# A dummy first activation, and all four units of the first attention group scored in plain fp32

## The chip, the cores and the metric

The kernel runs on one core of one Trainium2 chip. The metric is the device time of one execution in microseconds; three runs of the kernel before the change had a median of 709.19 us (709.08 to 709.35).

## The reference

Three stages follow each other. Attention with a memory is computed for 2 batches, 8 heads, 576 rows and 64 columns a head; its output goes through a dense layer with an ELU between two weights, and this through four experts, each weighted by a probability of the row.

```python
scores = scale * np.matmul(q, k.transpose(0, 1, 3, 2))
scores = np.where(causal, -1000000000.0, scores)
a = np.exp(scores - scores.max(-1, keepdims=True))
a /= a.sum(-1, keepdims=True) + 1e-09
local = np.matmul(a, v)
q_p = phi(q)                              # phi(x) = where(x > 0, x, exp(x) - 1) + 1
mem_out = (q_p @ M_prev) / (q_p @ z_prev + 1e-6)
attn = g * mem_out + (1 - g) * local      # g = sigmoid(beta), one a head
...
h = x @ w_in                              # 1152 x 512 by 512 x 2048
x = np.where(h > 0.0, h, np.exp(np.minimum(h, 0.0)) - 1.0) @ w_out
...
for e in range(E):                        # 4 experts, 512 x 1024 x 512
    out += p[:, e:e + 1] * (np.maximum(x @ w1[e], 0.0) @ w2[e])
```

## The kernel before, in words

All work is cut into steps, each with an engine, a cost, a rank and the steps that it needs. A planner (`Plan.order`) walks a model of the five engines when the program is built, and of the steps that could start on an engine it takes the one with the lowest rank; what comes out is a fixed order of instructions on each engine. On the chip each engine runs its order strictly, one instruction after the other, and waits on semaphores for what it needs. The table `MOVES` shifts ranks by step or by family of steps (`("R", "load")` is the load of all units of kind R, `"R00"` all steps of one unit). `STAY` says how far down the ranks TensorE looks for a step of the kind that it is at (attention or dense layers) before it turns to the other kind; its first number holds while it is at attention. Nothing of the planner's costs is a time of the chip.

Attention is done in units of a pair of heads. Four units `F0` to `F3` hold the first 192 rows of both batches (tiles 0 and 1, 192 keys wide, and tile 2, 64 wide); their output is the input of the first token group (384 rows) of the dense layers. Eight units `R00` to `R13` hold the rest (tiles 576, 448 and 320 keys wide), for the second group of 768 rows. The steps of a unit are:

- `load` and `load_v`: the queries with the keys (tile `qk`), and the values with the memory (tile `rv`), issued by SyncE;
- `split_h` on ScalarE and `split_l` on GpSimd: a high part `qh` in fp32r, the reduced-precision type, and the rest `ql`; a unit in `DIRECT` leaves them out;
- `phi_r`, `phi_e`, `phi_p` on ScalarE and `phi` on GpSimd (for R, `phi_p` is GpSimd's too): phi of the queries, then `mem` on TensorE into the bank `om`;
- `score` on TensorE: three products of the parts (high by high, low by high, high by low), or one in plain fp32 for a `DIRECT` unit; the two heads go to two PSUM banks;
- `lowest` on VectorE: mask and minimum, with the result in SBUF; `exp` on ScalarE; `trans` on TensorE, four blocks at a time into the one bank `t`; `evac` copies them to SBUF, on ScalarE for even groups and on VectorE for odd ones; `values` on TensorE into the bank `ov`; then the quotient on VectorE, the sum with the memory part, the turn on TensorE, and the split of the result as input of the dense layer.

The weights come as 64-bit words for the first dense layer (steps `upper` on ScalarE, `shift` and `lower` on VectorE, for each half of a weight, put the words back into fp32; for the first three weights these work in the tile `wr` in SBUF, for the others in a PSUM bank), and as fp32 for the experts; `part_h` on ScalarE and `part_l` on GpSimd split them into `wh` and `wl`. Each dense product is three fp32r products (`mm3`). Tiles go round in rings: two each of `raw`, `qh`, `ql` and `rv`, one of `om`, `ov` and `t`. A load into a ring waits until the last reader of the tile that it replaces is done. Seven fillers (products of zeros, L342) run first on TensorE, and some more where the planner sees a wait or a unit of kind F begins a group.

Of the kernel before, what the change touches and what calls it, by code (L numbers as in the profile page):

```python
# [8 lines left out]
F32 = mybir.dt.float32  # L9
F32R = mybir.dt.float32r  # L10
I32 = mybir.dt.int32
I64 = mybir.dt.int64
AF = mybir.ActivationFunctionType
# [3 lines left out]
B, H, S, D = 2, 8, 576, 64  # L17
# [3 lines left out]
P = 128  # L21
# [6 lines left out]
NQ = 384  # L28
# [4 lines left out]
KEYS = {"F": 192, "R": 576}  # L33
# [20 lines left out]


MOVES = {
# [11 lines left out]
}  # L68


# [14 lines left out]
def f32(ap):  # L85
    return ap.bitcast(F32)
# [3 lines left out]
def tile_kernel(  # L90
# [12 lines left out]
    nc = tc.nc  # L103
    qk, vm = {"F": qk_f, "R": qk_r}, {"F": vm_f, "R": vm_r}

    const = ctx.enter_context(tc.tile_pool(name="const", bufs=1))
# [29 lines left out]
    zeros = const.tile([P, P], mybir.dt.bfloat16, name="zeros")  # L136
    nc.vector.memset(zeros, 0.0)


    wmem = const.tile([P, H], F32, name="wmem")  # L140
    wloc = const.tile([P, H], F32, name="wloc")
# [63 lines left out]
    UNIT1 = 5.0  # L205

    LANDING = 1.2
    DIRECT = ("F0", "F1")
    EARLY = 4.0
    START2 = 48.0  # L210
    STARTS2 = [0, 35, 70, 95, 110, 125, 140, 155]
# [143 lines left out]
    def atile(shape, dtype, tag, name):  # L355
        return at["sbuf"].tile(shape, dtype, tag=tag, name=name, bufs=SLOTS[tag])
# [719 lines left out]
    def act_cost(n, psum=False):  # L1076
        return 0.833e-3 * n + (0.055 if psum else 0.095)
# [4 lines left out]
    def pool_cost(n):  # L1082
        return 2.1e-3 * n + 0.2
# [2 lines left out]

        return 0.06 * (kind == "F") + 0.203 * sum(2 if kind == "F" and (t, odd) == (2, 2) else 1 for t, odd, _ in blocks)

    STAY = [16.5, 17.0]
    TURN = 0.09  # L1090

    def attends(key):
# [117 lines left out]
    def plan_unit(plan, kind, b, c, start, spare, slack):  # L1210
# [5 lines left out]
        widest = 1344  # L1216
        unit, uid = {}, f"F{c}" if kind == "F" else f"R{b}{c}"

        def parts_of(t):

            if kind == "F":
                return [(t, 0, P)] if t < 2 else [(0, 0, D), (1, D, D)]
            return [(0, 0, P)]

        def add(key, engine, cost, fn, after=(), takes=(), gives=()):
            step = key.rstrip("0123456789")
            plan.add(
                (uid, key), engine, cost, start + OFFSET[step], fn,
                [(uid, a) if isinstance(a, str) else a for a in after], takes, gives,
                slack.get(engine, 0.0) + LANDING * (step in ("split_h", "phi_r") and uid not in ("F0", "F1")),  # L1230
                early=EARLY if kind == "R" else 1e9,
            )


        def load(cs):
            if "k" not in unit:
                unit["k"] = atile([P, NQ + KEYS["R"]], F32, tag="raw", name=f"qk{uid}")[:, :nq + nk]
            nc.sync.dma_start(out=unit["k"][:, cs], in_=(qk[kind][c] if kind == "F" else qk[kind][b, c])[:, cs])

        def load_v():  # L1240
# [31 lines left out]
        whole, direct = slice(0, nq + nk), uid in DIRECT  # L1272
        if uid == "F0":

            add("load_k", "sync", 0.8, lambda: load(slice(nq, nq + nk)), takes=["raw"])
            add("load_q", "sync", 0.5, lambda: load(slice(0, 2 * P)))
            add("load", "sync", 0.4, lambda: load(slice(2 * P, nq)))
        else:
            add("load", "sync", 1.6, lambda: load(whole), takes=["raw"])
        add("load_v", "sync", 1.3, load_v, takes=["rv"])  # L1280
        if not direct:
            n = nq + nk
            add("split_h", "act", act_cost(n), lambda: split_h(whole), ["load"], ["qh"])
            add("split_l", "pool", pool_cost(n), lambda: split_l(whole), ["split_h"], ["ql"])
        add("phi_r", "act", act_cost(nq), phi_r, ["load"], ["pp"])
        add("phi_e", "act", act_cost(nq), phi_e, ["phi_r"], ["pe"])
        if kind == "F":
            add("phi_p", "act", act_cost(nq), phi_p, ["phi_e"] + ["split_l"] * (not direct), gives=["raw"] * (not direct))
            add("phi", "pool", pool_cost(nq), phi, ["phi_p"] + ["score20"] * direct, gives=["pe"] + ["raw"] * direct)
        else:  # L1290
            add("phi_p", "pool", 2.5e-3 * nq + 0.2, phi_p, ["phi_e"])
            add("phi", "pool", pool_cost(nq), phi, ["phi_p", "split_l"], gives=["raw", "pe"])
# [108 lines left out]
            nc.scalar.activation(out=blk, in_=blk, func=AF.Exp, scale=-1.0, bias=unit["nm"][odd][:, k:k + 1])  # L1401

        def score_cost(t, w):
            return len(parts_of(t)) * max((4 if direct else 3) * w / 2400, 0.32) + 0.24 + 0.22 * FEWEST[kind] * (t != 1)

        for t, n, a, z_ in pieces:
            first, last = (t, n) == pieces[0][:2], (t, n) == pieces[-1][:2]
# [265 lines left out]
```

## Time and profile before

| | |
|---|---|
| median of 3 runs | 709.19 us |
| the profiled execution | 709.2 us |
| its span, first to last instruction | 707.4 us |
| TensorE busy | 696.5 us, 98% |
| GpSimd, VectorE, ScalarE busy | 424.3, 388.5, 350.9 us |
| granted TensorE clock over the span | 1.000 |

The span is the time between the first and the last instruction of the profiled execution; 1.8 us of its time lie around it. Busy times of the engines overlap. A matmul's end is modelled in the profile, so that consecutive matmuls overlap in the rows: the time from one start to the next is the better price. A bracket at the end of a row of the timeline holds the idle time before it and who ended it.

### The profile page before, as it was taken

Reading aid. Unit: us, or ns where it says so; the run is one execution under the profiler, and the core shown is the slowest. Engines: PE = TensorE matmul, PEld = TensorE weight load, DVE = VectorE, ACT = ScalarE, POOL = GpSimd, SP = SyncE. Lnnn points to the kernel's source line nnn. Section 1 sums busy time; section 2 is a strip of 40 time slices with the busy share of each in tenths; the row PEclk is TensorE's granted clock in tenths of the full one; section 3 lists DMA queues with packets and bytes.
Section 4 is the critical chain, followed back from the end, with each engine's and each line's share of the span. In section 5 each row is a group of like instructions: output and inputs, shape, how many; then the busy total and the mean of one; then the engine's idle time right before and its main releaser. Section 6 shows DMA issues by size and latency. Waiting matters only on the chain.

```text
span 707.4 us, 10617 instructions
## 1 busy us (share of the span) xinstructions
PE 696.5 (98%) x4043; PEld 636.6 (90%) x4043; DVE 388.5 (55%) x844; ACT 350.9 (50%) x607; POOL 424.3 (60%) x255
## 2 busy tenths in 40 slices
PE   8989999999999999999999999999999999999997
PEld 5778998899888898999999999999898989989896
DVE  3897787553445323523727557763554636355462
ACT  6878967664434523544855546733332424233220
POOL 4877767566553444598886464796645666464210
PEclk9999999999999999999999999999999999999999
DMA  7889986433322331234321202122220303111002
GB/s 275 281 273 306 311 301 223 173 99 109 117 93 63 118 116 63 90 120 156 111 77 60 90 30 62 60 91 81 66 90 30 120 11 110 58 62 60 0 1 89
DMA packets 23826, 82.19 MB, mean 116 GB/s; under 512 B 2912, under 2 KB 3296, under 8 KB 23776
## 3 DMA queue, kind: packets, MB, share of 16 engines
q1 hardware_dynamic: 23776, 81.53, 34.9%
q8 instruction: 31, 0.51, 0.3%
q14 instruction: 19, 0.16, 0.1%
HBM read 70.77 MB, written 10.75 MB: 115 GB/s over the span
## 4 chain that ended last, share of the span: by engine, by line
PE 83%; DVE 0%; issue 0%
PE db L318 9%; PE db L316 9%; PE db L317 9%; PE da L316 4%; PE da L318 4%; PE da L317 4%; PE ub L316 3%; PE ub L318 3%; PE ub L317 3%; PE ov L1457 3%; PE sR L1378 2%; PE tR L1441 2%; PE ov L1464 1%; PE pb17S L318 0%; PE pb16S L317 0%; PE pb15S L316 0%
## 5 line engine op out<-in xcount | busy, mean ns | idle before, releaser
L284 POOL TENSOR_TENSOR wl<-wr,wh 128x1024 fp32r<-128x1024 f32 x72 | 172.1, 2395 | 161.0 <-ACT wh L280 152.5
L280 ACT ACTIVATE wh<-wr 128x1024 fp32r<-128x1024 f32 x72 | 76.0, 1056 | 114.4 <-PE db L317 73.0
L316 PE MATMUL db<-wh,hb 128*128 128x512 f32 x288 | 112.8, 392 | 0.0
L318 PE MATMUL db<-wl,hb 128*128 128x512 f32 x288 | 112.5, 391 | 0.0
L317 PE MATMUL db<-wh,hb 128*128 128x512 f32 x288 | 112.4, 390 | 0.0
L1046 DVE SCALAR_TENSOR_TENSOR acc<-db,pr,acc 128x512 f32<-128x512 f32 x42 | 31.5, 751 | 70.8 <-PE db L318 70.8
L316 PE MATMUL da<-ha,wh 128*128 128x384 f32 x192 | 65.9, 343 | 0.0
L318 PE MATMUL da<-ha,wh 128*128 128x384 f32 x192 | 64.3, 335 | 0.0
L318 PEld LDWEIGHTS db<-wl,hb 128*128 128x128 f32 x288 | 54.0, 188 | 11.4
L317 PE MATMUL da<-ha,wl 128*128 128x384 f32 x192 | 64.2, 335 | 0.0
L316 PEld LDWEIGHTS db<-wh,hb 128*128 128x128 f32 x288 | 54.1, 188 | 10.7 <-issue 0.2
L317 PEld LDWEIGHTS db<-wh,hb 128*128 128x128 f32 x288 | 54.1, 188 | 10.7
L316 PE MATMUL ub<-yh,wh 128*128 128x384 f32 x128 | 45.2, 353 | 0.0
L318 PE MATMUL ub<-yl,wh 128*128 128x384 f32 x128 | 43.0, 336 | 0.0
L317 PE MATMUL ub<-yh,wl 128*128 128x384 f32 x128 | 43.0, 336 | 0.0
L1457 PE MATMUL ov<-rvR,pfR 128*128 128x65 f32 x288 | 38.5, 265 | 0.0
L1457 PEld LDWEIGHTS ov<-rvR,pfR 128*128 128x128 f32 x288 | 37.7, 191 | 0.7 <-issue 0.2
L554 ACT ACTIVATE hb<-ub 128x384 fp32r<-128x384 f32 x32 | 15.7, 491 | 43.5 <-PE ub L318 43.1
L316 PEld LDWEIGHTS da<-ha,wh 128*128 128x128 f32 x192 | 36.1, 188 | 1.0 <-issue 1.0
L557 DVE SCALAR_TENSOR_TENSOR hb<-ub,hb 128x384 fp32r<-128x384 f32 x32 | 17.7, 557 | 33.4 <-ACT hb L554 33.4
L317 PEld LDWEIGHTS da<-ha,wl 128*128 128x128 f32 x192 | 36.1, 188 | 0.0
L318 PEld LDWEIGHTS da<-ha,wh 128*128 128x128 f32 x192 | 36.0, 188 | 0.0
(859 smaller groups left out, 1820.6 us busy)
## 6 DMA issues: line engine op xcount, KB each, us to landing
wr<-in_w SPq DMA_DIRECT2D x64, 512.0 KB, 3.5
w<-in_w SPq DMA_DIRECT2D x32, 512.0 KB, 6.3
wscr<-wr SPq DMA_DIRECT2D x16, 512.0 KB, 7.2
wr<-wscr SPq DMA_DIRECT2D x16, 512.0 KB, 3.3
rvR<-in_vm_r SPq DMA_DIRECT2D x8, 520.0 KB, 4.5
qkR<-in_qk_r SPq DMA_DIRECT2D x8, 480.0 KB, 6.2
rvF<-in_vm_f SPq DMA_DIRECT2D x4, 520.0 KB, 5.0
out<-acc SPq DMA_DIRECT2D x8, 256.0 KB, 2.0
```

The costliest lines, as they stand in the source:

```text
L280: nc.scalar.activation(out=t["wh"], in_=t["wr"], func=AF.Copy)
L284: nc.gpsimd.tensor_tensor(out=wl, in0=t["wr"], in1=f32(t["wh"]), op=ALU.subtract)
L316: nc.tensor.matmul(out, ah, bh, start=first, stop=False)
L317: nc.tensor.matmul(out, al, bh, start=False, stop=False)
L318: nc.tensor.matmul(out, ah, bl, start=False, stop=last)
L554: nc.scalar.activation(out=t["h"][:, 0], in_=t["ps"], func=AF.Relu)
L557: nc.vector.scalar_tensor_tensor(out=t["h"][:, 1], in0=t["ps"], scalar=0.0, in1=f32(t["h"][:, 0]), op0=ALU.max, op1=ALU.subtract)
L1046: nc.vector.scalar_tensor_tensor(out=acc, in0=t["ps"], scalar=p, in1=acc, op0=ALU.mult, op1=ALU.add)
L1378: nc.tensor.matmul(unit["s", odd, t, n][:, :w], unit[x][rows, q], unit[y][rows, ks[odd]], start=m == 0 and r0 == 0, stop=m == len(terms) - ...
L1441: nc.tensor.transpose(pst[:, P * n:P * n + P], src, ident)
L1457: nc.tensor.matmul(unit["ov"][:, odd, t], pf[:, col:col + P], unit["rv"][:, at_], start=False, stop=odd == 1 and j == nb - 1)
L1464: nc.tensor.matmul(pair("ov", t, r0, r), pf[:, col + r0:col + r0 + r], apart(at_), start=True, stop=nb == 0,)
```

## The change

ScalarE gets a first operation, an exponential of one column of the tile of zeros that the fillers use. `F2` and `F3` join the units that score in plain fp32, so their `split_h` and `split_l` and their buffers `qh` and `ql` are not needed; their raw tiles (queries and keys) are laid into these two rings in place of `raw`. The planner's costs for these scores, two costs of phi on ScalarE, `STAY` and the whole table `MOVES` are changed with it, and so the order of the program on every engine.

```diff
 MOVES = {
-    ("F", "exp"): 15.5, ("F", "load"): -18.5, ("F", "trans"): 3, ("F0", "mem"): 5.5, ("F0", "values1"): 17,
...
+    ("F", "exp"): 9.8, ("F", "score"): -61.6, ("F", "turn"): 30.9, ("F1", "exp21"): -1.6,
...
+    awake = const.tile([P, 1], F32, name="awake")
+    nc.scalar.activation(out=awake, in_=zeros[:, :1], func=AF.Exp)
...
-    DIRECT = ("F0", "F1")
+    DIRECT = ("F0", "F1", "F2", "F3")
...
-    STAY = [16.5, 17.0]
+    STAY = [145.4, 17.7]
...
+        home = {"F2": "qh", "F3": "ql"}.get(uid, "raw")
...
-                unit["k"] = atile([P, NQ + KEYS["R"]], F32, tag="raw", name=f"qk{uid}")[:, :nq + nk]
+                block = atile([P, NQ + KEYS["R"]], F32 if home == "raw" else F32R, tag=home, name=f"qk{uid}")
+                unit["k"] = f32(block)[:, :nq + nk]
...
-            add("load", "sync", 1.6, lambda: load(whole), takes=["raw"])
+            add("load", "sync", 1.6, lambda: load(whole), takes=[home])
...
-        add("phi_e", "act", act_cost(nq), phi_e, ["phi_r"], ["pe"])
+        add("phi_e", "act", act_cost(nq) + 0.12, phi_e, ["phi_r"], ["pe"])
...
-            add("phi_p", "act", act_cost(nq), phi_p, ["phi_e"] + ["split_l"] * (not direct), gives=["raw"] * (not direct))
-            add("phi", "pool", pool_cost(nq), phi, ["phi_p"] + ["score20"] * direct, gives=["pe"] + ["raw"] * direct)
+            add("phi_p", "act", act_cost(nq) + 0.12, phi_p, ["phi_e"] + ["split_l"] * (not direct), gives=["raw"] * (not direct))
+            add("phi", "pool", pool_cost(nq), phi, ["phi_p"] + ["score20"] * direct, gives=["pe"] + [home] * direct)
...
-            return len(parts_of(t)) * max((4 if direct else 3) * w / 2400, 0.32) + 0.24 + 0.22 * FEWEST[kind] * (t != 1)
+            if direct:
+
+                cold = {0: 0.7, 1: 0.35}.get(t, 0.0) * (uid == "F0")
+                return len(parts_of(t)) * (0.32 if w > D else 0.25) + 0.12 + 0.05 * (t == 2) + 0.22 * FEWEST[kind] * (t != 1) + cold
+            return len(parts_of(t)) * max(3 * w / 2400, 0.32) + 0.24 + 0.22 * FEWEST[kind] * (t != 1)
```

ScalarE at the start of the program, before: `pp` and `pe` are the tiles of phi, `pt` holds scores and then exponentials, `pf` the copies of transposed blocks `t`; the name's first letters after it are the unit.

```order
L1257 ACT_TABLE_LOAD
L1257 ACTIVATE ppF0_155<-qkF0_139 128x448
L1261 ACTIVATE peF0_163<-ppF0_155 128x448
L1265 ACTIVATE ppF0_155<-qkF0_139 128x448
L1401 ACTIVATE ptF0_147<-ptF0_147,nmF00_148 128x192
L1257 ACTIVATE ppF1_180<-qkF1_143 128x448
L1401 ACTIVATE ptF0_147<-ptF0_147,nmF01_149 128x192
L1401 ACTIVATE ptF0_147<-ptF0_147,nmF00_148 128x192
L1401 ACTIVATE ptF0_147<-ptF0_147,nmF01_149 128x192
L1401 ACTIVATE ptF0_147<-ptF0_147,nmF00_148 128x64
```

The same place after the change:

```order
L143 ACT_TABLE_LOAD
L143 ACTIVATE awake_95<-zeros_93 128x1
L1266 ACTIVATE ppF0_157<-qkF0_141 128x448
L1270 ACTIVATE peF0_161<-ppF0_157 128x448
L1274 ACTIVATE ppF0_157<-qkF0_141 128x448
L1410 ACTIVATE ptF0_149<-ptF0_149,nmF00_150 128x192
L1410 ACTIVATE ptF0_149<-ptF0_149,nmF01_151 128x192
L1410 ACTIVATE ptF0_149<-ptF0_149,nmF00_150 128x192
L1410 ACTIVATE ptF0_149<-ptF0_149,nmF01_151 128x192
L1266 ACTIVATE ppF1_188<-qkF1_147 128x448
```

The table load stands at an operation on the zeros, F0's four 192-wide exponentials follow each other, and the first step of F1's phi has gone behind them. The copy `pfF00` (not in these rows) stands two exponentials and no other step further down.

SyncE's issues, from the first half of weight 0 on, before (`w64_i_h` is half h of weight i):

```order
L246 DMA w64_0_0_183<-in_w64 128x512
L1238 DMA qkF2_208<-in_qk_f 128x832
L246 DMA w64_0_1_230<-in_w64 128x512
L246 DMA w64_1_0_252<-in_w64 128x512
L1238 DMA qkF3_267<-in_qk_f 128x832
L246 DMA w64_1_1_290<-in_w64 128x512
L1242 DMA rvF2_315<-in_vm_f 128x1040
L1238 DMA qkR00_330<-in_qk_r 128x960
```

And after:

```order
L1247 DMA qkF2_182<-in_qk_f 128x832
L252 DMA w64_0_0_200<-in_w64 128x512
L1247 DMA qkR00_229<-in_qk_r 128x960
L252 DMA w64_0_1_242<-in_w64 128x512
L1251 DMA rvF2_264<-in_vm_f 128x1040
L171 DMA pr_99<-in_probs 128x36
L1247 DMA qkR10_298<-in_qk_r 128x960
L1247 DMA qkF3_322<-in_qk_f 128x832
```

F2's load and R00's have moved up, F3's has moved back behind R10's and F2's values, and weight 1 (not in these rows) comes behind F3.

VectorE around the minimum steps of unit R00, before: the rows `ISA pt...` are the minimum steps (each with a second row that reads out the minimum), `L270` is `lower`, `sR00001` and `sR00101` the scores of the second piece of the widest tile:

```order
L1392 ISA ptR00_537,nmR000_538<-sR00001_577,mask_71,nmR000_538 128x288
L1392 ISA nmR000_538 128x1
L1392 ISA ptR00_537,nmR001_539<-sR00101_578,mask_71,nmR001_539 128x288
L1392 ISA nmR001_539 128x1
L270 SCALAR_TENSOR_TENSOR wr1_324<-w64_1_1_290,wr1_324 128x512
L266 TENSOR_SCALAR cv3_0_599<-cv3_0_599 128x512
L270 SCALAR_TENSOR_TENSOR wr3_598<-w64_3_0_426,cv3_0_599 128x512
L1300 SCALAR_TENSOR_TENSOR nv_F3_630<-ov_121,wloc_96 128x6
```

And after:

```order
L1401 ISA ptR00_479,nmR000_480<-sR00001_523,mask_71,nmR000_480 128x288
L1401 ISA nmR000_480 128x1
L1401 ISA ptR00_479,nmR001_481<-sR00101_524,mask_71,nmR001_481 128x288
L1401 ISA nmR001_481 128x1
L1459 COPY pfF31_550<-tF31_537 128x384
L272 TENSOR_SCALAR wr1_461<-wr1_461 128x512
L276 SCALAR_TENSOR_TENSOR wr1_461<-w64_1_0_350,wr1_461 128x512
L1401 ISA ptR00_479,nmR000_480<-sR00010_555,mask_71 128x448
```

Behind the same minimum steps there stood three steps of weights, F3's quotient and more before R00's 448-wide piece (`sR00010`); now there stand one copy and two steps of weight 1, whose first half comes later than it did, and then that piece.

## Rows read from the trace of the kernel before

**Rows 1.** The page: span and TensorE's busy time, share and instructions.

```profile
span 707.4 us, 10617 instructions
PE 696.5 (98%) x4043; PEld 636.6 (90%) x4043; DVE 388.5 (55%) x844; ACT 350.9 (50%) x607; POOL 424.3 (60%) x255
```

**Rows 2.** Windows: length, busy PE, PEld, DVE, ACT, POOL, clock, DMA share, GB/s.

```profile
0.00:5.00 5.00, 4.03 (x12) 1.54 (x14) 0.11 (x1) 0.00 (x0) 3.20 (x14) 1.00 0.52 136
5.00:30.00 25.00, 23.30 (x195) 16.80 (x191) 16.47 (x72) 23.18 (x51) 14.44 (x9) 1.00 0.88 299
30.00:60.00 30.00, 27.23 (x203) 23.33 (x202) 26.96 (x64) 24.54 (x46) 24.18 (x18) 1.00 0.87 285
60.00:120.00 60.00, 58.31 (x383) 55.07 (x382) 47.36 (x101) 48.17 (x84) 43.19 (x27) 1.00 0.85 293
120.00:700.00 580.00, 580.00 (x3247) 537.15 (x3245) 296.14 (x606) 255.03 (x429) 339.30 (x190) 1.00 0.25 81
700.00:707.40 7.40, 3.63 (x17) 2.66 (x15) 1.50 (x2) 0.00 (x0) 0.00 (x0) 1.00 0.26 99
```

**Rows 3.** Timeline of ScalarE: start, duration, line, operation, tiles, count, idle before.

```profile
5.37 1.28 ACT L1257 ACT_TABLE_LOAD   x1 [5.37 <-DMA qkF<-in_qk_f]
6.66 0.58 ACT L1257 ACTIVATE ppF<-qkF 128x448 f32<-128x448 f32 x1
...
8.36 0.44 ACT L1401 ACTIVATE ptF<-ptF,nmF 128x192 f32<-128x192 f32 x1
```

**Rows 4.** Timeline of TensorE, units F0 and F1.

```profile
7.69 0.81 PE L342 MATMUL sF<-zeros 128*128 128x512 bf16 x3 [0.43 <-DVE nmF L1392]
8.43 0.92 PE L1378 MATMUL sF<-qkF 64*128 64x192 f32 x8
9.28 0.39 PE L342 MATMUL tF<-zeros 128*128 128x512 bf16 x1
9.75 0.93 PE L1441 MATMUL tF<-ident,ptF 128*128 128x128 f32 x4
...
13.08 0.49 PE L1464 MATMUL ov<-rvF,pfF 128*128 128x130 f32 x2 [0.72 <-ACT pfF L1448]
```

**Rows 5.** Timeline of ScalarE and GpSimd: split of a unit, one each.

```profile
15.00 0.88 ACT L1247 ACTIVATE qhF<-qkF 128x832 fp32r<-128x832 f32 x1
...
23.66 1.95 POOL L1252 TENSOR_TENSOR qlF<-qkF,qhF 128x832 fp32r<-128x832 f32 x1
```

**Rows 6.** Timeline of TensorE: F2's 192-wide scores from parts, and what follows.

```profile
21.24 0.36 PE L1378 MATMUL sF<-qhF 64*128 64x192 f32 x2
...
22.08 0.61 PE L342 MATMUL om<-zeros 128*128 128x512 bf16 x2
```

**Rows 7.** Timeline of TensorE: F2's turn and two long waits.

```profile
35.76 0.49 PE L1502 MATMUL xF<-ident,tvF 128*128 128x128 f32 x3
...
39.63 0.47 PE L1378 MATMUL sR<-qhR 64*128 64x448 f32 x2 [1.34 <-DVE wr L270]
...
51.21 0.66 PE L1441 MATMUL tR<-ident,ptR 128*128 128x128 f32 x4 [1.43 <-DVE pfR L1446]
```

**Rows 8.** Timeline of VectorE: `lower` of weights in SBUF.

```profile
35.75 2.43 DVE L270 SCALAR_TENSOR_TENSOR wr<-w,wr 128x512 int32<-128x512 int32 x1
...
45.21 2.63 DVE L270 SCALAR_TENSOR_TENSOR wr<-w,wr 128x512 int32<-128x512 int32 x1
...
48.53 0.69 DVE L270 SCALAR_TENSOR_TENSOR wr<-w,wr 128x512 int32<-128x512 int32 x1
```

**Rows 9.** Timeline of GpSimd: subtractions beside the two slow steps.

```profile
35.38 2.25 POOL L1252 TENSOR_TENSOR qlR<-qkR,qhR 128x960 fp32r<-128x960 f32 x1
...
45.03 2.27 POOL L1252 TENSOR_TENSOR qlR<-qkR,qhR 128x960 fp32r<-128x960 f32 x1 [2.33 <-ACT qhR L1247]
```

**Rows 10.** DMA issues from 0 to 40 us: size, median us to landing.

```profile
w<-in_w SPq DMA_DIRECT2D x10, 512.0 KB, 6.6
...
qkF<-in_qk_f SPq DMA_DIRECT2D x3, 416.0 KB, 4.0
```

More of the change, by code (lines that the diff above doesn't have):

```diff
@@ L1273, in plan_unit @@
         if uid == "F0":
-            add("load_k", "sync", 0.8, lambda: load(slice(nq, nq + nk)), takes=["raw"])
+            add("load_k", "sync", 0.8, lambda: load(slice(nq, nq + nk)), takes=[home])
             add("load_q", "sync", 0.5, lambda: load(slice(0, 2 * P)))
```

23 rows, old and new, of the table MOVES are left out of this document.

## The prediction

> **What bounds the kernel now.** I read the page first, then the table of windows, then the timelines of the first 60 us. TensorE is busy for 696.5 of the span's 707.4 us [rows 1], so the time can fall only where TensorE stands idle, or where its own work shrinks. The windows say where it stands idle [rows 2]: 0.97 us before 5 us (nothing to multiply yet), 1.70 us between 5 and 30, 2.77 between 30 and 60, 1.69 between 60 and 120, nothing from 120 to 700, and 3.77 at the end, where the last sums are formed and stored. What can be won are the middle three, 6.16 us. In 5 to 30 us ScalarE is the busiest engine beside TensorE (23.2 of 25 us), and the DMA engines run at 0.88; from 30 to 60 us VectorE is (27.0 of 30) [rows 2].
>
> The profiled execution took 709.2 us, that is 1.8 us around its span of 707.4 [rows 1]; the median of the timed runs is 709.19, so the same sum serves for both. What tells this kernel from no change is about 0.2%, 1.4 us.
>
> **The change, part by part.**
>
> *ScalarE's first operation.* Now ScalarE loads its table when its first operation's data have landed, at 5.37 us, for 1.28 us, and the first activation begins at 6.66 [rows 3]. The new operation reads a tile of zeros that VectorE sets at the start, so the table load goes into time in which ScalarE has nothing else to do, and the first activation can begin at 5.37. Gain on ScalarE: 1.28 us. The Trainium skill ("ScalarE: Activation LUTs", What ACT_TABLE_LOAD costs) adds a drain of about 1.38 us to a load of 1.28; here the activation follows the load at once, so the trace does not agree, and with the drain the sum would fall by up to 1.4 us more.
>
> What waits for it: F0's transposes on TensorE, which now start at 9.75 us [rows 4] behind F0's exponentials. In the new order the four exponentials stand in a row behind the three steps of phi. The first went at 8.36 [rows 3], so now at about 7.1; four of 0.44 us end by 8.8 at the latest, and the transposes can start at about 8.9, some 0.9 us sooner. But F1's scores, which stood ahead of these transposes (8.43 to 9.28 us), come behind them now. F0's scores end at 7.26 (7.69 less the 0.43 of waiting [rows 4]); two fillers follow, some 0.25 us each by the three that take from 7.69 to 8.43, and then TensorE idles from 7.7 to 8.9, about 1.2 us. Behind that the 0.72 us at 13.08 [rows 4], a wait for the copy of F0's transposes, should go: this copy is ScalarE's next step but two behind the exponentials. The walk down the new order gives about 1.2 us of idle time for 5 to 30 us in place of 1.70: **-0.5** (bounds: all 1.7 gone; or F0's transposes as late as now with nothing ahead of them, +0.9, which is 9.75 less 8.9).
>
> *F2 and F3 score in plain fp32.* Off TensorE, each drops one ScalarE copy of 0.88 us and one GpSimd subtraction of 1.95 us [rows 5], so F2's scores wait for its load alone. On TensorE a pair of 192-wide tiles goes from 12 reduced-precision products to 4 plain ones. The 12 take from 21.24 to 22.08, 0.84 us [rows 6]; F1's 4 plain ones take from 8.43 to 9.28, 0.85 us [rows 4], at the full clock (1.00, 2.4 GHz [rows 2]). I take the cost as zero. It lies on the bounding engine, with no cover: if a group's price were wrong by 0.1 us, the four such groups of F2 and F3 (a 192-wide and a 64-wide one in each) would add 0.4. The Trainium skill ("FP8 and Floating Point Precision", TensorE Precision Notes) speaks against the change: true fp32 makes four passes through the array, while the split form makes three products. By that rule these four groups, at 0.84 us or less each, would cost up to a third more, at most 1.1 us, and the sum would be 707.9; the rows agree with no such loss, so I keep zero.
>
> *The raw tiles in the place of the split parts.* F2's load waited for F0's raw tile; its new buffer is free from the start, so its issue moves up in the queue. F0's values now come ahead of F1's keys, so F1 lands later by about the time of one more transfer (520 KB at the 299 GB/s of that window, 1.8 us [rows 2]); its cover is that F1's scores stand behind F0's transposes now. Without the cover the 1.8 us would be TensorE's. F3's load stands behind R10's, which needs F1's raw tile, and so F1's last scores: a new wait, and a rival below.
>
> *The new order between 30 and 60 us.* This is the largest term. The two long idle stretches are 1.34 us at 39.63 and 1.43 at 51.21 [rows 7]. Both stand behind VectorE's step `lower` of an early weight, which took 2.43 us at 35.75 and 2.63 at 45.21, while the same step on the same shape took 0.69 at 48.53 [rows 8]. What differs is GpSimd: its subtractions of 2.25 and 2.27 us run at just those times [rows 9]. Such a stretch costs VectorE 1.7 to 1.9 us, and the minimum step behind it holds the PSUM banks of R00's next scores. In the new order the first of these `lower` steps stands ahead of the minimum steps of R00's 448-wide piece, not behind the scores that wait for them; between those scores and the next there stand F2's turn, F3's last values and six products of the first layer, which now take from 35.76 to 38.29 us (39.63 less the wait [rows 7]), so 1.9 us of lateness is covered. The next two (weight 2) stand before the copy of R00's second transposes; there the cover is less, about 1 us. That GpSimd lost two subtractions of 2 us before this point makes a collision less likely, not impossible. I take one collision, half covered: 0.9 us of idle time in place of 2.77, **-1.9** (bounds: -2.8 with none; +2.7 with three uncovered, as the first rival has it).
>
> *60 to 120 us.* The order changes there too: units R00 to R11 are more tightly packed, since the kernel stays with attention as long as a step is ready. I found no wait there that goes or comes for certain, and take the 1.69 us as they are: **0** (bounds -1.7 to +1.7, none or twice as much). Entering another kind of product costs TensorE little: I count 56 entries of the dense layers from the plain fp32 products before and 48 now, and the scores' entries stay about as many; I take zero, within 0.5.
>
> *The rest of the table.* From 120 to 700 us TensorE has no idle time [rows 2], so reordering weights there is covered by TensorE itself; the end is not touched.
>
> Sum: 709.2 - 0.5 - 1.9 = **706.8 us**.
>
> **The rivals.**
>
> *VectorE falls under GpSimd (slower).* The place is the three `lower` steps in SBUF ahead of R00's minimum steps and transposes. If all three run beside a GpSimd subtraction, they cost 1.74, 1.94 and about 1.84 more, 5.5 us in all; if the tighter attention leaves TensorE nothing else to do, idle time between 30 and 60 us is 5.5 in place of my 0.9, and the time is 706.8 + 4.6 = 711.4. It is slower from 4.7 us of uncovered lateness on (710.6). For it: two of such steps fell so in the profile. Against: GpSimd has less to do before. Chance 0.13.
>
> *The waits only change place (no change).* Attention in a row makes a chain transposes, copy, values with one transposition bank; each link waits for a copy, and 6.2 us of idle time comes back elsewhere: 709.2. For it: TensorE's work stays the same, and VectorE was busy for nine tenths of 30 to 60 us. Chance 0.19.
>
> *F3's load is late.* By the walk its issue is at about 15 us, behind F1's last scores, and its own scores are due at 22. Such loads took 4.0 us to land, weights' 6.6 [rows 10]; beyond 7 us each further us is idle. At 10 us of landing it costs 3 and the time is 709.8; chance 0.05, half of it within the bound and half above it.
>
> *More than forecast.* All idle time between 5 and 120 us goes: 709.2 - 6.2 = 703.0. Chance 0.09; it asks that no collision is left.
>
> **How the numbers follow.** The forecast, 704.5 to 708, has 0.54. Faster: 0.54 + 0.09 = 0.63. Same: 0.19 and half of 0.05, 0.21. Slower: 0.13 and the other half, 0.16. The range runs from 702.9, which leaves out the lowest few of a hundred, to 710.6, above which lie most of the first rival and little else. For the forecast alone the range is 704.5 to 708.
>
> **What would show it.** Right: the table load ends before 3 us and the first activation begins at about 5.4; F0's transposes begin at 8.7 to 9.1; F2's and F3's pairs of 192-wide scores take 0.8 to 0.9 us; TensorE's idle time is about 1.2 between 5 and 30 us, and about 1 between 30 and 60, with its busy time within 1 us of 696.5. Wrong: a wait of over 1 us on VectorE's `lower` or on a copy of transposes between 30 and 65 us; a wait of F3's scores on its load at 22 us; idle time of over 3 us between 60 and 120 us, where I walked nothing; or scores in plain fp32 over 1 us a pair.

## The result, and the profile after

The changed kernel takes 702.25 us (median of 5 runs, 702.08 to 703.13), before 709.19 in the same session: ratio 0.9904, 95% interval 0.989 to 0.9919. It is faster, as forecast, but by 7 us where 2.4 were forecast, and 0.65 us below the wider of its two ranges (702.9 to 710.6).

The page of after, first line and engines, as [rows 1]:

```profile
span 700.3 us, 10577 instructions
PE 694.2 (99%) x4028; PEld 636.1 (91%) x4028; DVE 383.9 (55%) x844; ACT 349.2 (50%) x606; POOL 418.2 (60%) x253
```

The windows of after, columns as in [rows 2]:

```profile
5.00:30.00 25.00, 23.62 (x194) 16.93 (x192) 17.30 (x79) 22.15 (x52) 12.61 (x9) 1.00 0.91 305
30.00:60.00 30.00, 30.00 (x221) 26.38 (x218) 25.78 (x73) 25.18 (x46) 21.86 (x17) 1.00 0.88 290
60.00:120.00 60.00, 60.00 (x409) 56.84 (x408) 48.27 (x105) 47.56 (x84) 40.89 (x26) 1.00 0.85 296
```

TensorE's idle time went from 1.70 to 1.38 us (5 to 30 us), from 2.77 to 0 (30 to 60) and from 1.69 to 0 (60 to 120): 4.78 us. Its busy time fell by 2.35, from 696.5 to 694.15. Together that is the 7.1 us by which the span is shorter.

ScalarE's and TensorE's timelines of after at the start, as [rows 3, 4]:

```profile
0.72 1.28 ACT L143 ACT_TABLE_LOAD   x1 [0.72 <-PEq L1676]
2.01 0.20 ACT L143 ACTIVATE awake<-zeros 128x1 f32<-128x1 bf16 x1
5.38 0.58 ACT L1266 ACTIVATE ppF<-qkF 128x448 f32<-128x448 f32 x1 [3.16 <-DMA qkF<-in_qk_f]
7.08 1.48 ACT L1410 ACTIVATE ptF<-ptF,nmF 128x192 f32<-128x192 f32 x4
```

```profile
4.39 0.92 PE L1387 MATMUL sF<-qkF 64*128 64x192 f32 x8
8.01 0.93 PE L1454 MATMUL tF<-ident,ptF 128*128 128x128 f32 x4 [0.94 <-ACT ptF L1410]
...
20.00 0.66 PE L1387 MATMUL sF<-qkF 64*128 64x64 f32 x8
20.59 0.66 PE L1470 MATMUL ov<-rvF,pfF 128*128 128x65 f32 x4
...
22.53 0.92 PE L1387 MATMUL sF<-qkF 64*128 64x192 f32 x8
23.38 0.39 PE L348 MATMUL om<-zeros 128*128 128x512 bf16 x1
```

The table load lies in idle time, F0's transposes begin at 8.01 instead of 9.75 us [rows 4], and a pair of 192-wide plain fp32 scores of F3 takes 0.85 us from start to start (22.53 to 23.38), against 0.84 for the three products of parts [rows 6]. A pair of 64-wide ones takes 0.59 us (F2's, 20.00 to 20.59); before, F2's from parts took 0.79, from the first of these rows to the second:

```profile
24.44 0.30 PE L1378 MATMUL sF<-qhF 64*128 64x64 f32 x2
...
25.23 0.39 PE L342 MATMUL tF<-zeros 128*128 128x512 bf16 x1
```

VectorE's `lower` steps in SBUF, and GpSimd's timeline around them, as [rows 8, 9]:

```profile
34.03 0.69 DVE L276 SCALAR_TENSOR_TENSOR wr<-w,wr 128x512 int32<-128x512 int32 x1
36.65 0.69 DVE L276 SCALAR_TENSOR_TENSOR wr<-w,wr 128x512 int32<-128x512 int32 x1
43.32 0.68 DVE L276 SCALAR_TENSOR_TENSOR wr<-w,wr 128x512 int32<-128x512 int32 x1
44.38 0.69 DVE L276 SCALAR_TENSOR_TENSOR wr<-w,wr 128x512 int32<-128x512 int32 x1
```

```profile
32.72 1.00 POOL L1279 TENSOR_TENSOR ppR<-peR,ppR 128x384 f32<-128x384 f32 x1
37.04 1.33 POOL L1276 TENSOR_SCALAR ppR<-qkR 128x384 f32<-128x384 f32 x1 [3.32 <-ACT peR L1270]
38.52 2.39 POOL L290 TENSOR_TENSOR wl<-wr,wh 128x1024 fp32r<-128x1024 f32 x1
40.86 1.01 POOL L1279 TENSOR_TENSOR ppR<-peR,ppR 128x384 f32<-128x384 f32 x1
45.86 1.16 POOL L1276 TENSOR_SCALAR ppR<-qkR 128x384 f32<-128x384 f32 x1 [3.99 <-ACT peR L1270]
```

Almost all of each `lower` step falls into GpSimd's two gaps (to 37.04 and to 45.86 us), and all take 0.68 to 0.69 us. No collision of a `lower` step is left there, and neither are the waits of 1.34 and 1.43 us [rows 7].

### The profile page after: what moved, and what is told of

It reads as the page before. It is cut to its first block, busy times and chain, and to the rows that moved or that the text cites. A ratio compares the mean times of both kernels' runs of the same rounds, so it can differ in the third digit from the quotient of the medians.

```text
span 700.3 us, 10577 instructions
## 1 busy us (share of the span) xinstructions
PE 694.2 (99%) x4028; PEld 636.1 (91%) x4028; DVE 383.9 (55%) x844; ACT 349.2 (50%) x606; POOL 418.2 (60%) x253
## 4 chain that ended last, share of the span: by engine, by line
PE 97%; ACT 1%; DMA 1%; DVE 0%; SPq 0%; issue 0%; ACTq 0%
PE db L322 9%; PE db L324 9%; PE db L323 9%; PE da L322 5%; PE da L324 5%; PE da L323 5%; PE ov L1470 5%; PE ub L322 3%; PE ub L324 3%; PE ub L323 3%; PE sR L1387 3%; PE tR L1454 3%; PE ua L322 2%; PE ua L324 2%; PE ua L323 2%; PE ov L1477 1%
## 5 line engine op out<-in xcount | busy, mean ns | idle before, releaser
L1410 ACT ACTIVATE ptR<-ptR,nmR 128x576 f32<-128x576 f32 (+2 forms) x48 | 29.8, 662 | 11.3 <-DVE nmR L1401 11.2
```

## The experiments

The kernels whose expectations were worked out against the changed kernel's 702.25 us are compared with it by their medians; the ratios are against the kernel before, run in the same session each time. By the intervals of the ratios a difference of two medians is uncertain by 1 to 1.5 us, so that a difference of 1 us or less is an indication only.

**The dummy activation alone, in the kernel before.**

```diff
+    awake = const.tile([P, 1], F32, name="awake")
+    nc.scalar.activation(out=awake, in_=zeros[:, :1], func=AF.Exp)
```

> The kernel before, with only the dummy first activation added; the order of everything else is as before. Theory A (the new order made the gain; the table load alone is worth what TensorE's start waits for): F0's transposes start up to 0.25 us sooner, since F1's scores still stand ahead of them until 9.28 us and a filler behind, and the 0.72 us wait at 13.08 shrinks; the time is 708.0 to 709.0. Theory B (ScalarE was the bound of the first 30 us, so what is taken off it comes through in full): 1.28 us and more, 707.9 or less.

Measured: 707.98 us, ratio 0.9982 (0.9971 to 0.9994). The whole schedule moves up by about 1 us; both long waits stand where they stood in the order, and as long:

```profile
38.57 0.47 PE L1381 MATMUL sR<-qhR 64*128 64x448 f32 x2 [1.36 <-DVE wr L273]
50.12 0.66 PE L1444 MATMUL tR<-ident,ptR 128*128 128x128 f32 x4 [1.43 <-DVE pfR L1449]
```

By the ratio the early load brings 1.3 us (0.4 to 2.1), about its own length; the time lies at the border of the two theories.

**A collision taken out of the kernel before.** GpSimd waits with a subtraction until VectorE is past a `lower` step.

```diff
+            if (i, half) in ((1, 1), (2, 0)):
+                nc.vector.memset(flag[:, :1], 0.0)
...
+            if uid in ("R10", "R01"):
+                nc.gpsimd.tensor_copy(flag[:, 1:], flag[:, :1])
```

> The kernel before, with GpSimd's subtractions for R10 and R01 made to wait for the `lower` step of VectorE that they ran beside (weight 1's second half, weight 2's first), by a flag of one column that VectorE sets behind it; no step is moved. Theory A (the two long waits of TensorE came from these two slow steps): both steps take 0.7 us, the waits of 1.34 and 1.43 us shrink by 1.3 each at most, and the time is 706.5 to 708. Rival (VectorE was late for other reasons, or GpSimd's later end costs as much): 708.7 to 710.

Measured: 707.53 us, ratio 0.9971 (0.9961 to 0.9982). VectorE's first flagged `lower` step, and the step behind the second:

```profile
36.24 0.69 DVE L272 SCALAR_TENSOR_TENSOR wr<-w,wr 128x512 int32<-128x512 int32 x1
...
45.32 2.76 DVE L272 SCALAR_TENSOR_TENSOR wr<-w,wr 128x512 int32<-128x512 int32 x1
```

The first is free and its wait of 1.34 us is gone; at the second the subtraction, now from 45.28 us on, only met the next `lower` step, and 1.27 us of waiting stays. One collision removed is worth 2 us (1.3 to 2.7): its wait of 1.34 us, and a rest that this run does not explain.

**The split work put back, unread, in the changed kernel**: both halves, ScalarE's alone, GpSimd's alone. The order of everything else is that of the changed kernel, and nothing is left out.

```diff
+            if uid in ("F2", "F3"):
+                nc.scalar.activation(out=scratch, in_=unit["k"], func=AF.Copy)
...
+            if uid in ("F2", "F3"):
+                nc.gpsimd.tensor_tensor(out=scratch, in0=unit["k"], in1=scratch, op=ALU.subtract)
```

> The changed kernel, in the same order, with the split work of F2 and F3 put back as work whose result nobody reads: a ScalarE copy of 832 columns ahead of phi_r, and a GpSimd subtraction of 832 columns ahead of phi, for each of the two units. TensorE still scores from the raw tile. Theory A (order): this work had slack in the new order; the time is 702.2 to 703.3. Theory B (less work on ScalarE and GpSimd made the gain): 0.88 us on ScalarE and 2 us on GpSimd come back twice, and TensorE idles between 15 and 35 us: 704.5 to 707.

> The changed kernel with one ScalarE copy 832 wide put back for F2 and for F3, whose result nothing reads (the GpSimd half of the dropped split stays away). Both halves together took 704.3 us. Theory A (ScalarE was the engine that mattered: its queue stands ahead of the exps and copies that TensorE waits for): 703.5 to 704.5 us. Theory B (GpSimd's subtractions mattered, they delay what VectorE and TensorE need): 702.0 to 702.8 us.

> The changed kernel with one GpSimd subtraction 832 wide put back for F2 and for F3, whose result nothing reads (no copy on ScalarE). Theory A (ScalarE was the engine that mattered): 702.0 to 702.8 us. Theory B (GpSimd's subtractions mattered): 703.5 to 704.5 us, with waits of TensorE behind GpSimd, or behind VectorE where a step with two SBUF operands meets the subtraction.

Measured: 704.28 (ratio 0.9928, 0.9913 to 0.9943), 703.27 (0.9918, 0.9903 to 0.9933) and 703.76 us (0.9925, 0.991 to 0.994). The first lies just under B, the second between its theories, the third in B. ScalarE's half costs 1.0 us, of which its profile shows 0.47 as a late load (below), GpSimd's 1.5, of which 0.84, and both 2.0, of which 0.91. VectorE beside GpSimd with both halves:

```profile
20.06 1.76 DVE L273 TENSOR_SCALAR wr<-wr 128x512 int32<-128x512 int32 x1
21.86 1.50 DVE L277 SCALAR_TENSOR_TENSOR wr<-w,wr 128x512 int32<-128x512 int32 x1
```

```profile
19.59 1.95 POOL L1283 TENSOR_TENSOR scratch<-qkF,scratch 128x832 f32<-128x832 f32 x1
21.49 1.32 POOL L1284 TENSOR_TENSOR ppF<-peF,ppF 128x448 f32<-128x448 f32 x1
```

The same two steps with ScalarE's half alone:

```profile
20.06 0.95 DVE L273 TENSOR_SCALAR wr<-wr 128x512 int32<-128x512 int32 x1
21.05 0.69 DVE L277 SCALAR_TENSOR_TENSOR wr<-w,wr 128x512 int32<-128x512 int32 x1
```

So a subtraction that the change drops would itself be a collision in the new order: the shift meets it, `lower` meets the addition that it has delayed, VectorE is 1.6 us later, and TensorE, about to score F3, waits 1.08 us at 23.56 behind F2's last minimum step. ScalarE's half alone brings neither. This is weight 0, in the first 30 us. Between 30 and 60 us, where the collisions of the kernel before were, the kernel with both halves put back has almost no idle time on TensorE, and of its `lower` steps of weights 1 and 2 only the first is slow, beside an addition (ScalarE's half alone makes it as slow):

```profile
30.00:60.00 30.00, 29.73 (x219) 25.58 (x217) 25.34 (x70) 26.44 (x50) 22.47 (x16) 1.00 0.82 266
```

```profile
35.58 1.38 DVE L277 SCALAR_TENSOR_TENSOR wr<-w,wr 128x512 int32<-128x512 int32 x1
38.89 0.69 DVE L277 SCALAR_TENSOR_TENSOR wr<-w,wr 128x512 int32<-128x512 int32 x1
```

**Collisions put back at weights 1 and 2 of the changed kernel.**

```diff
+            if 0 < i < W_EARLY:
+                nc.vector.memset(flag[:, :1], 0.0)
+                nc.gpsimd.tensor_copy(flag[:, 1:], flag[:, :1])
+                nc.gpsimd.tensor_tensor(out=scratch, in0=wide, in1=wide, op=ALU.subtract)
```

> The changed kernel, but for weights 1 and 2 VectorE sets a flag ahead of each `lower` step, and GpSimd, which waits for that flag, runs a subtraction of two 896-wide SBUF tiles beside it (its result is read by nothing). In the trace of before a `lower` step beside such a subtraction took 2.4 to 2.6 us in place of 0.69. Theory A (the collisions on VectorE were priced rightly, and the new order has no cover for them): the `lower` steps of the two weights become 2.4 to 2.7 us, TensorE waits again behind VectorE between 30 and 60 us, 703.5 to 706 us. Theory B (the new order leaves VectorE enough slack, the collisions of before mattered only because other work was late there): the steps are just as long, TensorE does not wait, 702.0 to 703.0 us.

Measured: 703.78 us, ratio 0.9915 (0.9898 to 0.9933). The waits of TensorE that it brought:

```profile
PE ua L330 <- POOL wl L297: 0.9, 1, 0.9
PE da L330 <- POOL wl L297: 0.2, 1, 0.2
```

The time is A's, the mechanism is not: three of the four `lower` steps take 1.0 to 2.1 us (less than the 2.4 to 2.7 that were meant), and TensorE never waits for VectorE there. The cover that the prediction counted (the six products and F3's last values) was enough for these; what is late is GpSimd's own `wl`, behind the added work in its queue.

**One half of the change each: the old table and `STAY` with four units in plain fp32, and the new table with two; and the new table with the old `STAY`.**

```diff
-    STAY = [145.4, 17.7]
+    STAY = [16.5, 17.0]
...
-    DIRECT = ("F0", "F1", "F2", "F3")
+    DIRECT = ("F0", "F1")
```

> The changed kernel with the table and the STAY of the kernel before: fp32 scores in all four units, the dummy activation and the new homes stay, the scheduler orders them by the old numbers (62 filler matmuls where the changed kernel has 36). Theory A (the removed work and the early table load bring the larger half of the 7 us whatever the order): 703 to 705.5 us. Theory B (the new order brings the larger half): 706 to 709 us, with waits of TensorE of 3 us or more between 5 and 120 us.

> The changed kernel with its new table and its dummy activation, but F2 and F3 split again as before, their raw tiles in the raw buffers. The scheduler, told of the splits, makes its own order from the same table (54 filler matmuls where the changed kernel has 36). Theory A (the removed split work on ScalarE and GpSimd is what leaves the stretch from 5 to 120 us without waits; an order can't hide it): waits of 2 to 4 us come back there, 704.5 to 707 us. Theory B (the table does it, fp32 scores are a by-product): no more than 703.5 us.

> The new table with F2 and F3 split, again, for its profile (the first look fell into a disturbed execution). Its time was 716.0 us, 14 more than the changed kernel. Theory A (it is fillers and waits: the scheduler foresees that TensorE waits for the splits): 54 fillers where the changed kernel has 25 to 36, idle time of TensorE from 5 to 120 us above 3 us, both together above 8 us. Theory B (work moved past 120 us, transfers or evictions late there): idle time after 120 us above 3 us.

> The changed kernel with one number put back: STAY = [16.5, 17.0] in place of [145.4, 17.7], which moves a few rows of the order. Theory A (the gain lies in the removed work and the table, this number is of no weight): 701.6 to 703.0 us, no wait of TensorE over 0.5 us beyond those of the changed kernel. Theory B (the order is balanced so finely that any change of it brings waits): 703.5 to 706 us.

Measured: 714.54 us (ratio 1.007, 1.0054 to 1.0086) for the old table; 716.04 (1.0087, 1.0069 to 1.0105) and, run again, 716.92 for two units; 702.87 (0.9904, 0.9889 to 0.992) for the old `STAY`. All times forecast for the first two were too low: each half by itself is slower than before, by 5 and 7 us. The windows with the old table:

```profile
5.00:30.00 25.00, 22.63 (x179) 16.20 (x176) 16.66 (x74) 21.89 (x49) 9.33 (x7) 1.00 0.91 314
30.00:60.00 30.00, 26.91 (x185) 20.48 (x184) 23.56 (x60) 19.80 (x36) 20.93 (x14) 1.00 0.79 270
```

Idle time between 5 and 60 us is 5.5 us, and the planner, which foresaw part of the waits, put in 62 fillers where the changed kernel has 36 and the one before 35: 26 more at 0.22 us each, the step between fillers, are 5.7 us of TensorE. A collision comes back here although F2 and F3 are not split: GpSimd's subtraction for an R unit meets a `lower` step.

```profile
38.48 2.22 POOL L1258 TENSOR_TENSOR qlR<-qkR,qhR 128x960 fp32r<-128x960 f32 x1
39.10 2.15 DVE L273 SCALAR_TENSOR_TENSOR wr<-w,wr 128x512 int32<-128x512 int32 x1
```

With two units it is 54 fillers and 6.4 us of idle time between 5 and 120 us, 3.44 of it one wait for exponentials at 21.46. The table fits the four fp32 units, and only these; the old `STAY` costs 0.6 us, and its profile shows 0.58 us of waiting for the load told of below.

**The dummy activation taken out of the changed kernel**, and that with 8 fillers in place of 2 ahead of F0's first transposes.

```diff
-    awake = const.tile([P, 1], F32, name="awake")
-    nc.scalar.activation(out=awake, in_=zeros[:, :1], func=AF.Exp)
...
-            keep_busy(pst, FEWEST[kind])
+            keep_busy(pst, 8 if (uid, g) == ("F0", 0) else FEWEST[kind])
```

> The changed kernel without the dummy first activation. Both theories: the table load stands in front of F0's phi again, F0's exponentials end 1.28 us later, and TensorE, which has nothing else there, waits 0.94 + 1.28 = 2.2 us for them. If nothing behind has slack to give back, the time is 702.25 + 1.28 = 703.5. If the waiting is made good later (TensorE is never idle behind it, so it should not be), 702.3 to 702.8.

> The changed kernel without the dummy activation, and with 8 filler matmuls in place of 2 ahead of F0's first transposes, so that TensorE waits there about 0.4 us where without them it waited 1.69 us. Without the dummy activation alone the kernel took 705.1 us, 2.9 more than the changed one, and its profile showed a granted clock at half from 8.95 to 15.77 us. Theory A (the late table load itself costs 1.3 us, and the rest of the 2.9 is the clock, lost in the long wait): the clock stays full after its first rise, 703.3 to 704.3 us. Theory B (the 2.9 us are all lateness of ScalarE's exps, and the half clock hid inside waits): 704.8 to 706 us, whether the clock falls or not.

Measured: 705.12 us (ratio 0.9942, 0.9925 to 0.9958) and 704.42 (0.9933, 0.9916 to 0.9949). The windows of the first show the granted clock (the column 1.00, 0.50):

```profile
5.00:9.00 4.00, 2.41 (x19) 1.34 (x15) 1.62 (x12) 3.57 (x6) 0.41 (x1) 0.99 0.92 329
9.00:15.70 6.70, 6.42 (x26) 4.26 (x27) 2.10 (x10) 5.11 (x15) 1.86 (x2) 0.50 0.71 280
15.70:30.00 14.30, 14.20 (x121) 10.51 (x121) 11.24 (x51) 10.76 (x24) 7.57 (x5) 1.00 0.77 242
```

F0's transposes wait 1.69 us, the clock falls to half in that wait, and F1's scores and F0's values run at 1.2 GHz. With the fillers the wait is 1.05 us and the clock stays at 1.00. The first time is above both of its forecasts, the second between its two theories, and both profiles had another wait: TensorE for the values (`rv`) of the third R unit, 0.64 and 0.83 us.

**That load taken out of the way.** A third buffer for `rv`, so that the load is issued at 52.7 us instead of 56.3; room from the buffers of memory sums (`tm`) or of transposed scores (`ph`). The order is unchanged on every engine.

```diff
-        return at["sbuf"].tile(shape, dtype, tag=tag, name=name, bufs=SLOTS[tag])
+        return at["sbuf"].tile(shape, dtype, tag=tag, name=name, bufs={"rv": 3, "ph": 3}.get(tag, SLOTS[tag]))
```

> The changed kernel with a third buffer for the units' value tiles (and one for the memory sums where there were two, to make room); the order on every engine is unchanged. The load of the third R unit's values, which waits until 56.3 us for a buffer, can go at about 53 us. In the profile of the changed kernel it landed 4.1 us after its issue and just in time (60.39 us, needed at 61.44); in seven other profiles it landed 5.6 to 6.1 us after, 0.5 to 0.9 us too late. Theory A (this load is the next limit, and shows in part of the executions): the wait is gone, 701.3 to 702.3 us. Theory B (the one buffer for the memory sums makes VectorE wait, or the earlier load delays the weights behind it): 702.5 to 704 us.

> The same as the run before with the room taken from the transposed-score buffers (three where there were four) and two for the memory sums as before. Theory A: 701.3 to 702.3 us. Theory B (a copy of transposes waits for its buffer): 702.5 to 704 us, with a wait of TensorE behind such a copy.

Measured: 706.51 us with one `tm` (ratio 0.9953, 0.9941 to 0.9966), 701.94 with three `ph` (0.9899, 0.9884 to 0.9913). The first is above both of its theories. The second keeps the gain and has no wait of TensorE over 0.2 us between 5 and 690 us; it is 0.3 us under the changed kernel, which these intervals can't tell from the same. One `tm` costs a wait at 165 us, where GpSimd's reading of the one buffer holds up VectorE:

```profile
162.31 0.33 PE L322 MATMUL ub<-yh,wh 128*128 128x384 f32 x1
162.48 0.34 PE L323 MATMUL ub<-yh,wl 128*128 128x384 f32 x1
164.97 0.44 PE L324 MATMUL ub<-yl,wh 128*128 128x384 f32 x1 [2.15 <-DVE yl L510]
```

The two undone parts were then run again with that load early. The first two (with one `tm`, for room) carry the 4 us of that buffer, 706.85 and 707.18 us, and tell nothing of the parts; the two after them took the room from `ph` alone.

> The changed kernel with the unread copy on ScalarE and the unread subtraction on GpSimd for F2 and F3 (784 of 832 columns wide, for room), and the third buffer for value tiles (one for memory sums, three for transposed scores). Without that buffer the unread split work made it 704.3 us, 2.0 more than the changed kernel, of which the profile showed 0.9 as a wait for the values' load. Theory A (the split work itself costs about 1.1 us, the load the rest): 703.0 to 703.7 us. Theory B (the split work costs all of the 2 us): 704.0 to 705 us.

> The changed kernel without the dummy activation, with 8 fillers ahead of F0's first transposes, and with the third buffer for value tiles. Without that buffer it was 704.4 us, of which the profile showed 0.83 as a wait for the values' load. Theory A (the late table load costs its 1.3 us and the load's wait made up the rest): 703.2 to 703.8 us. Theory B (the late table load costs 2 us or more by itself): 704.1 to 705 us.

> The changed kernel without the dummy activation, with 8 fillers ahead of F0's first transposes, and with the third buffer for value tiles, the room taken from the transposed-score buffers (the one buffer for memory sums had cost 4 us by itself; this way of making room costs nothing: 701.9 us with the dummy activation). Theory A (the late table load costs its 1.3 us, and the load's wait made up the rest of the 2.2): 702.8 to 703.5 us. Theory B (the late table load costs 2 us or more by itself): 703.9 to 705 us.

> The changed kernel with the unread copy on ScalarE and the unread subtraction on GpSimd for F2 and F3 (816 of 832 columns, written as 16-bit numbers, for room) and the third buffer for value tiles, the room taken from the transposed-score buffers. Theory A (the split work costs about 1.1 us, a wait of VectorE's minimum step ahead of F3's turn, and the load's wait made up the rest of the 2.0): 702.6 to 703.4 us. Theory B (the split work costs all of the 2 us): 703.6 to 704.6 us.

Measured for the last two: 703.16 us without the dummy activation (ratio 0.9915, 0.9902 to 0.9929), 704.0 with the split work (0.9926, 0.9913 to 0.994). Against 701.94 the early table load is worth 1.2 us (A: its own length, so the rest of the 2.9 goes with the clock and the load's wait, which were not told apart further), and the dropped split work 2.1 us (B: all of it). In the last kernel the shift takes 1.57 us beside GpSimd's subtraction and `lower` again 1.50 beside the addition behind it, and TensorE waits 0.90 us at 23.61 for the same minimum step.

## Why the prediction was wrong

The direction was right, and so was the mechanism of its largest term: TensorE waited for VectorE's slow `lower` steps, and these waits went. Three steps failed, and their misses all point the same way: "I take one collision, half covered: 0.9 us" (none came), the zero for 60 to 120 us (1.69 us went), and TensorE's busy time taken as the same "within 1 us of 696.5" (it fell by 2.35).

*5 to 30 us*, forecast -0.5: the idle time fell by 0.32, close. But the table load is worth about 1.2 us, measured alone in either order. Idle time in this window is not the measure of it: with the dummy activation alone TensorE's idle time between 5 and 120 us fell by 0.32 us, and its busy time by 0.9 (to 695.6). The marks were right (load over at 2.00 us, first activation at 5.38), except that F0's transposes came at 8.01, not 8.7 to 9.1: the four exponentials in a row take 1.48 us together, not four times 0.44.

*Plain fp32 in F2 and F3*, forecast zero on TensorE: right for the 192-wide pairs, 0.85 us each. The prediction read no row of a 64-wide pair; each of these takes 0.2 us less than from parts. The rule of four passes (the Trainium skill, "FP8 and Floating Point Precision", TensorE Precision Notes) would have made these pairs up to a third longer; the trace does not show it. Nor does the drain beside a table load (the Trainium skill, "ScalarE: Activation LUTs", What ACT_TABLE_LOAD costs) appear: `awake` begins 0.01 us after the load ends.

*30 to 60 us*, forecast -1.9, measured -2.77. The step "I take one collision, half covered: 0.9 us" failed. The prediction took collisions for a matter of chance and said that GpSimd's two lost subtractions make one "less likely, not impossible". The runs show that the order decides this stretch, not the two subtractions. The collisions of before were with subtractions of R10 and R01, which the change keeps. With F2's and F3's split work put back in the new order this stretch stays almost free of waits (0.27 us idle); with it dropped under the old table a `lower` step collides again (2.15 us). In the new order GpSimd has almost nothing to do at the times of `lower` there. What the dropped split work is worth, 2.0 to 2.1 us, it is worth elsewhere: at 20 to 23 us, where its subtraction would hold up VectorE and then TensorE. In that stretch the prediction counted no collision, with or without it.

*60 to 120 us*, forecast zero because "I found no wait there that goes or comes for certain": measured -1.69. This stretch was not walked, and the chain of waits there was in plain view. From 60 to 120 us in the kernel before, waits of TensorE:

```profile
PE sR L1378 <- DVE wr L270: 1.4, 3, 0.8
PE om L1325 <- DMA rvR<-in_vm_r: 0.3, 1, 0.3
```

The scores of the R units wait there for a PSUM bank in which a weight is being put together. After, who waited for `lower` from 60 to 125 us:

```profile
POOL qlR L1261: 5.3, 1
ACT wh L286: 4.5, 3
ACT cv L266: 2.4, 2
PEld sR L1387: 0.2, 1
```

TensorE's matmuls are not in it. In every kernel that the planner ordered anew these waits are gone, with the old table and four fp32 units too (0.26 us idle there in all), and what idle time there is in the others of the changed kernel is that of the values' load. So it is the order and not one part; which row of the table does it was not tried. The load of values was in time in the changed kernel's profile by luck: it landed 4.1 us after its issue; in six of the seven variants of the changed kernel with this order or nearly and two buffers it was 5.6 to 6.1, and 0.5 to 0.9 us too late.

*TensorE's busy time*, forecast within 1 us of 696.5: measured 694.15, the largest miss. Three things are in it. By the clock records of the traces TensorE's granted clock rose to full at 5.81 us before and at 4.22 after (a window counts the time ahead of the first record as full), so that F0's first eight score matmuls took 1.55 us before (from 4.49) and 0.92 after (the row at 4.39 above): 0.6 us. This is a matter of the execution and not of the change: in the profiles of the kernels here the rise came between 3.71 and 6.78 us. In the kernel with three `rv` and three `ph`, in the same order, it came at 6.45, and TensorE was busy for 695.0 us and waited 0.16 us for F0's exponentials instead of 0.94, in a span of 700.1 us. Second, the two 64-wide pairs took 0.4 us less. Third, a wait costs more than its idle time: in the rows at 162 to 165 us above the next matmul starts 2.49 us after the last, where the step is 0.17, so the wait costs 2.32 us and shows 2.15; the rest lies under the modelled end. Between 5 and 120 us there were 13 gaps of TensorE before and 4 after; nine times 0.17 us is 1.5. This share is an estimate, not tried by itself.

The sum for the two profiles: 4.78 us of idle time, 0.6 of clock, 0.4 of narrow scores and about 1.5 of hidden ends make 7.3, where 7.1 were measured. By parts: 1.2 us the table load, 2.1 the split work, and some 3.7 left by difference for the order (the collisions of 30 to 60 us, the waits of 60 to 120) with the narrow scores. The order can't be had alone: the new table without the four fp32 units is 7 us slower than before.

The rivals: "More than forecast" (703.0, chance 0.09) is what came true, and a little more. "VectorE falls under GpSimd" had the mechanism that matters with its sign turned round, and where it was forced at weights 1 and 2 the price came through GpSimd's queue. "The waits only change place" and "F3's load is late" did not show.

## What to carry to other kernels

Before pricing a collision as luck, ask which instruction makes it, whether the change removes that instruction or moves it, and what then runs beside each of the other engine's steps, from the start of the program on: work that leaves an idle-looking engine can be the wait of another. Time at the lower clock at the start differs from execution to execution; set it aside before two busy times are compared. Where the idle time of the bounding engine is listed by stretch, walk every stretch, and add to each wait the part that lies under the modelled end of the matmul before it. A tuned order fits one set of costs: with half of the change either way it was slower than no change.

## What the runs showed of the hardware

- The granted clock fell from 2.4 to 1.2 GHz in or soon after single waits of TensorE: in the wait of 1.69 us without the dummy activation, in that of 3.44 us with two fp32 units, and behind one of 2.15 us with one `tm` (from 166.3 us on a step took 0.32 us in place of 0.17); behind the same 2.15 us with the split work put back it stayed, and so it did over 1.05 us. Its first rise to full came between 3.71 and 6.78 us, TensorE being busy from 0.97 us on.
- A shift on VectorE from SBUF to SBUF (128x512) also slows beside GpSimd: 0.38 to 0.43 us alone, 0.95 to 1.36 with an addition beside most of it, 1.39 to 1.76 beside the subtraction put back for F2. A `lower` step that reads the weight's high part from a PSUM bank kept its 0.67 to 0.70 us beside GpSimd.
- A pair of plain fp32 scores took as long as its three fp32r products from parts at 192 keys (0.85 and 0.84 us), and less at 64 (0.59 and 0.79).
- The same load of values took 4.1 to 6.1 us from issue to landing in the same place of the order.
